# Reordering the end of a transformer prologue: K chunk 2, pair 7's transposes, V tile 1, and the idle products

## The chip, the cores and the metric

The kernel runs on one core of a Trainium2 chip. The metric is the device time of one execution in microseconds, here as the median of several executions. A core has five engines that run their own instruction queues: TensorE (PE, matmuls and transposes), VectorE (DVE), ScalarE (ACT, activations and copies), GpSimd (POOL) and SyncE (SP, which issues transfers).

## The reference

One pre-layernorm transformer block on x of 2048 rows by 512, in bfloat16, with 32 heads of 16 and a gated feed-forward layer of width 1792:

```python
def _A_ref(x, wqkv, wo):                     # H = 32, Dh = 16
    q, k, v = split_heads(x @ wqkv)
    p = softmax(einsum("bhqd,bhkd->bhqk", q, k) * Dh ** -0.5)
    return merge_heads(einsum("bhqk,bhkd->bhqd", p, v)) @ wo

def _B_ref(x, w_gate, w_up, w_down):
    return (sigmoid(x @ w_gate) * (x @ w_up)) @ w_down

h = x + _A_ref(layernorm(x), wqkv, wo)
out = h + _B_ref(layernorm(h), w_gate, w_up, w_down)
```

## The kernel before

The kernel has a prologue, a main loop over groups of score tiles, and a tail for the last query chunk's feed-forward layer.

The main loop (`emit_scores`, `emit_pv`, `emit_fill`) goes through groups of three score tiles of 128 keys by 512 queries. A group's scores are made by TensorE in one of two score buffers of three PSUM banks each, `pss0` and `pss1` in turn; ScalarE takes the exponential of the three banks in one instruction (line L887 in the profile), in some groups VectorE takes one tile of the three (L906 to L919). The product with V (L958) follows some groups later. Between the groups a generator, the filler, hands out the rest of the work one product at a time: V tiles 2 to 15 (L166), the K and Q projections of the other head groups (L171), the output projection and the feed-forward layer. In its first part the filler's V tiles go through two banks, the spare bank (`ps_misc`) and `acc`.

The softmax subtracts no maximum; it subtracts an upper bound of each score, from the norms of q and the largest norm of k. For the first two groups the bound is added to the scores by a second set of three products (L866) with `bnd`; later groups get it as further rows of `QB`, moved there by transfers (L248).

The prologue makes what the first groups need. x arrives in 16 tiles of 128 rows; they are treated in pairs, 0 to 7. For a pair u, `stats(u)` and `apply(u)` normalize on VectorE and GpSimd, `trans(u)` transposes by eight TensorE transposes into one bank and one ScalarE copy into `xnT` (L339, L341). K of head group 0 is made in chunks of 512 rows from two pairs each (`k_chunk`, `k_mm`, L171): a ScalarE square (`square`, L345) for the norms, a ScalarE evacuation into `stg` (`k_copy`, L361), and a transfer that spreads it into `KT` (`k_spread`, L221). The last chunk comes in two halves of 256 rows, half 6 from pair 6 and half 7 from pair 7 (`k_half`, L376; evacuations `half_copy`, L366), so that half 6 does not wait for pair 7. Pair 7's transposes go to two banks, one copied by VectorE, one by ScalarE (`transpose4`, L162, L163). The norms of K chunks 0 to 2 are collected in the spare bank (`norm_part_of`, L350), those of the halves come separately (`norm_half`, L385); `k_max` (L179) reduces each, `k_fold` (L189) and `k_most` bring them together, and `sqrt_bits` and one VectorE instruction make `bnd` (L461). V tiles 0 and 1 are also made here (`v_prod`, L166; `v_cast`, L227).

Three things set the order of the work. The schedule is manual: each engine runs its instructions in the order of the source, and only waits for data and for buffers lie between them. Until the prologue ends, its tiles take six PSUM banks in turn (`pm_tile`); the two score buffers lie on the same six banks, so the first scores wait for the last readers of the prologue's tiles. The spare bank and `acc` are outside of them. And three calls of `spin` (L253) issue TensorE products whose result nobody reads: two before K half 7, two before the last norm, five between group 0's scores (L861) and group 0's bounds (L866).

Of the kernel before, what the change touches and what calls it, by code (L numbers as in the profile page):

```python
# [11 lines left out]
FP32 = mybir.dt.float32  # L12
BF16 = mybir.dt.bfloat16
# [6 lines left out]
def kernel(  # L20
# [11 lines left out]
    nc = tc.nc  # L32
    P = 128
# [8 lines left out]
    QC = 512  # L42
# [24 lines left out]
    ps_misc = ctx.enter_context(tc.tile_pool(name="ps_misc", bufs=1, space=PSUM))  # L67
# [3 lines left out]
    def pm_tile():  # L71
        return pmh["pool"].tile([P, 512], FP32, name="pm")
# [6 lines left out]
    xnT = reg[:, 0:DC * S].rearrange("p (c s) -> p c s", c=DC)  # L79
# [6 lines left out]
    for part in (1, 0, 2):  # L86
        nc.sync.dma_start(out=wqkv_sb[:, :, part * D:(part + 1) * D],
                          in_=wqkv_v[:, :, part * D:(part + 1) * D])
# [7 lines left out]
    ident_bf = const.tile([P, P], BF16)  # L96
# [20 lines left out]
    acc = ps_acc.tile([P, QC], FP32, name="acc")  # L117
# [41 lines left out]
    def transpose4(dst3, src, copy=None):  # L159
        pt = pm_tile()[:].bitcast(BF16)[:, 0:4 * P].rearrange("p (b q) -> p b q", b=4)  # L160
        for b in range(4):
            nc.tensor.transpose(out=pt[:, b, :], in_=src[:, b * P:(b + 1) * P], identity=ident_bf[:])  # L162
        (copy or nc.vector.tensor_copy)(out=dst3, in_=pt)  # L163
# [14 lines left out]
    def k_max(src, dst):  # L178
        nc.vector.tensor_reduce(out=dst[0:src.shape[0], :], in_=src, axis=AX.X, op=ALU.max)  # L179
# [7 lines left out]
    def k_fold(kd, n, col):  # L187
        pc = ps_misc.tile([P, 512], FP32, name="pm")
        nc.tensor.matmul(pc[:, 0:4], lhsT=same[0:n].rearrange("p r h -> p (r h)"), rhs=kd[0:n, :],  # L189
                         start=True, stop=True)  # L190
        k_max(pc[:, 0:4], km2[:, col:col + 1])

    def k_most():
        m2 = small.tile([P, 1], FP32, name="m2")
        nc.vector.tensor_reduce(out=m2[:], in_=km2[:], axis=AX.X, op=ALU.max)
        return m2
# [10 lines left out]
    def q_root(ps, qc):  # L207
        r = slice(32 * qc, 32 * qc + 32)
        sqrt_bits(y0[r, :], ps[r, :])
# [10 lines left out]
    def k_spread(ku, g, cols, eng):  # L220
        eng.dma_start(out=KT[0:P:2, g, cols], in_=ku[64 * (g % 2):64 * (g % 2) + 64, cols])  # L221
# [29 lines left out]
    def spin(ps, rhs, n):  # L251
        for _ in range(n):
            nc.tensor.matmul(ps[:], lhsT=ident_bf[:], rhs=rhs, start=True, stop=True)  # L253
# [10 lines left out]
    def prologue(pro):  # L264
# [12 lines left out]
        for b in range(4):  # L277
            nc.vector.tensor_copy(out=ones_blk[:, b, :, 8 * b:8 * b + 8],
                                  in_=head_of[:].unsqueeze(1).to_broadcast([P, 4, 8]))
# [10 lines left out]
        means, rss, xns, pts, sqs = {}, {}, {}, {}, {}  # L290
# [44 lines left out]
        def trans(u):  # L335
            pts[u] = pm_tile()[:].bitcast(BF16).rearrange("p (b q) -> p b q", b=4)
            for i in range(2):
                for b in range(4):
                    nc.tensor.transpose(out=pts[u][:, b, i * P:(i + 1) * P],  # L339
                                        in_=xns[u][:, i, b * P:(b + 1) * P], identity=ident_bf[:])  # L340
            nc.scalar.copy(out=xnT[:, :, 2 * u * P:(2 * u + 2) * P], in_=pts[u])  # L341

        def square(key, ps, scale=1.0):
            sqs[key] = pro.tile([P, ps.shape[-1]], BF16, name="sq", bufs=3)
            nc.scalar.activation(out=sqs[key][:], in_=ps, func=ACT.Square, scale=scale)  # L345
# [13 lines left out]
        def k_copy(n, ps):  # L359
            cols = slice(n * QC, (n + 1) * QC)  # L360
            nc.scalar.copy(out=ku[:, cols], in_=ps[:])  # L361
            k_spread(ku, 0, cols, nc.sync)

        def half_copy(h):
            w = QC // 2
            nc.scalar.copy(out=ku[:, 3 * QC + h * w:3 * QC + (h + 1) * w], in_=ps3[h][:, 0:w])  # L366
# [3 lines left out]
            square(n, ps[:])  # L370
            k_copy(n, ps)

        def k_half(u):
            ps = pm_tile()
            for c in range(DC):
                nc.tensor.matmul(ps[:, 0:QC // 2], lhsT=wqkv_sb[:, c, D:D + P],  # L376
                                 rhs=xnT[:, c, u * QC // 2:(u + 1) * QC // 2], start=(c == 0), stop=(c == DC - 1))
            square(("half", u), ps[:, 0:QC // 2])
            return ps

        def norm_half(pn, u):
            norm_mm_to(pn[:, 0:QC // 2], sqs[("half", u)])
# [44 lines left out]
        stats(7)  # L427
        apply(6)
        norm_part_of(1)
        trans(6)  # L430
        ps2 = k_mm(2)
        square(2, ps2[:])
        q_root(acc, 0)
        apply(7)
        v1 = v_prod(1, pm_tile())
        norm_part_of(2)
        km4 = small.tile([P, 1], FP32, name="km4")
        k_max(pnp[0:96, :], km4)
        ps3 = [k_half(6)]
        for i, copy in enumerate((nc.vector.tensor_copy, nc.scalar.copy)):  # L440
            t = NT - 2 + i
            transpose4(xnT[:, :, t * P:(t + 1) * P], xns[7][:, i, :], copy)
        kd = k_spots(km4, 96)
        spin(acc, xnT[:, 0, 0:QC], 2)
        ps3.append(k_half(7))
        pn3 = pm_tile()
        norm_half(pn3, 6)
        k_max(pn3[:, 0:QC // 2], km2[:, 1:2])
        k_fold(kd, 96, 0)
        half_copy(1)  # L450
        v_cast(1, v1)
        half_copy(0)
        k_spread(ku, 0, slice(3 * QC, S), nc.sync)
        k_copy(2, ps2)
        spin(acc, xnT[:, 0, 0:QC], 2)
        pn3 = ps_misc.tile([P, 512], FP32, name="pm")
        norm_half(pn3, 7)
        k_max(pn3[:, 0:QC // 2], km2[:, 2:3])
        m2 = k_most()
        sqrt_bits(z0[:], m2[:])  # L460
        nc.vector.tensor_scalar(out=bnd[0:32, :], in0=y0[0:32, :].bitcast(FP32), scalar1=z0[0:32, :].bitcast(FP32),  # L461
# [26 lines left out]
    def v_prod(t, ps):  # L488
        for c in range(DC):
            v_mm(ps, t, c)  # L490
        return ps

    def v_cast(t, ps):
        v_store(t, ps, nc.scalar.copy)
        ready.add(("v", t))
# [351 lines left out]
    def emit_scores(i):  # L847
        group = groups[i]
        n = len(group)
        pss = pss2[i % 2]  # L850
        idle = i >= 3 * FIRST and (state["done"] or state["wait"] > i + CYC)
        pairs = i < FIRST or (i % 2 == 1 or i - i % CYC + 2 in twice) and not idle
        order = list(enumerate(group))
        if pairs and group[0][3] // 2 == group[1][3] // 2:
            order[1:] = order[:0:-1]
        n_of = max(per_bank(u[0]) for u in group)
        parts = [(ui, u, h) for h in range(n_of) for ui, u in order[:2] if h < per_bank(u[0])]
        parts += [(ui, u, h) for ui, u in order[2:] for h in range(per_bank(u[0]))]
        if i < OB:
            for ui, (c, g, k, j) in enumerate(group):  # L860
                nc.tensor.matmul(pss[:, ui, :], lhsT=KT[:, g, k * P:(k + 1) * P], rhs=QB[1][:, j, :],  # L861
                                 start=True, stop=False)
            if i == 0:
                spin(acc, xnT[:, 0, 0:QC], 5)
            for ui, (c, g, k, j) in enumerate(group):
                nc.tensor.matmul(pss[:, ui, :], lhsT=ident_bf[:, j:j + 1].to_broadcast([P, P]), rhs=bnd[:],  # L866
                                 start=False, stop=True)
            parts = []
        for ui, (c, g, k, j), h in parts:
            n_qg = c * NG + g  # L870
            w = CHUNKS[c][1]
            kt = k * per_bank(c) + h
            assert ("k", g // 2) in ready
            h0 = 64 * (j // 2)
            rows = slice(h0, h0 + 64) if pairs else slice(0, P)
            nc.tensor.matmul(pss[:, ui, h * w:(h + 1) * w], lhsT=KT[rows, g, kt * P:(kt + 1) * P],  # L876
                             rhs=QB[n_qg % 2][rows, j, 0:w], start=True, stop=True,
                             tile_position=(h0, 0) if pairs else None)
        for c, g, k, j in group:
            n_qg = c * NG + g  # L880
            if k == (12 if per_bank(c) == 1 else 0) and j == 3 and n_qg + 1 < len(qgs):
                emit_q_rows(n_qg + 1)
                emit_q_bound(n_qg + 1)
        slot = i % 7
        pt = pt4[slot] if slot < 4 else (pt_early if i < GM else pt_late)[slot - 4]
        na = n - 1 if i in split else n
        ex = nc.scalar.activation(out=pt[:, 0:na, :], in_=pss[:, 0:na, :], func=ACT.Exp, scale=DH ** -0.5 / QS)  # L887
        if na < n:
            scratch = scratch_of(i)
            tc.declare_no_dep(exp_bits(pss[:, na, :], *scratch).ins, ex.ins,  # L890
                              reason="both only read, from different banks")
            later(i + 1, lambda: exp_first(*scratch))
            later(i + 2, lambda: exp_second(*scratch))
            later(i + 3, lambda: exp_third(pt[:, na, :], *scratch))
        for ui, u in enumerate(group):
            p_of[u] = pt[:, ui, :]
# [210 lines left out]
```

## Time and profile before

| | |
|---|---|
| median of 3 executions | 961.85 us (961.81 to 962.77) |
| the profiled execution's own time | 963.82 us |
| its span, first to last instruction | 962.0 us |
| mean granted TensorE clock | 0.996 |
| TensorE busy | 843.0 us (88%) |
| VectorE busy | 782.9 us (81%) |
| ScalarE busy | 898.6 us (93%) |
| GpSimd busy | 39.8 us (4%) |
| first exponential of the main loop starts | 31.53 us |

Times in the profile count from the span's start. A row of a timeline gives the start, the duration, the engine, the line of the source, the operation, the tiles written and read, the shape, and how many instructions were merged; in brackets stand the idle time of the engine before it and what ended that. TensorE's records overlap, because products are pipelined. A stretch's row gives each engine's busy time in it and the clock that TensorE was granted, 1.00 being full speed.

### The profile page before, as it was taken

What the parts mean: (1) busy time and instruction counts of PE and PEld (TensorE: products, weight loads), DVE (VectorE), ACT (ScalarE), POOL (GpSimd) and SP (SyncE); (2) the same over time, 40 slices, a digit from 0 to 9 for tenths busy, and PEclk for the clock granted to TensorE, in tenths of its full rate; (3) what the DMA queues carried; (4) which work ended last, traced back from release to release, by engine and by line L of the source; (5) the groups of instructions that cost most, each with busy time, mean ns of one, the idle gap of its engine ahead of it and who ended that gap; (6) DMA issues with size and microseconds to landing.
All of it is one profiled execution on the core that took longest, in us unless ns stands there. A gap on an engine that the chain in (4) does not pass through costs nothing.

```text
span 962.0 us, 17291 instructions
## 1 busy us (share of the span) xinstructions
PE 843.0 (88%) x6442; PEld 337.0 (35%) x6442; DVE 782.9 (81%) x1413; ACT 898.6 (93%) x778; POOL 39.8 (4%) x56
## 2 busy tenths in 40 slices
PE   5998888878888999998788999988788999998988
PEld 2321222222222232222222223222355545456646
DVE  7488888888788888899888888898898778777643
ACT  6789999999999999999999999999998999999862
POOL 4600000000000000000000000000000000000000
PEclk9998999999999999999999999999999999999999
DMA  5102450000003000001001000000010000110010
GB/s 161 24 1 56 115 117 16 16 16 3 15 26 103 16 16 17 19 14 30 9 26 27 16 17 15 19 10 27 16 31 23 17 10 16 27 32 16 9 35 12
DMA packets 37645, 28.45 MB, mean 30 GB/s; under 512 B 17788, under 2 KB 32920, under 8 KB 37560
## 3 DMA queue, kind: packets, MB, share of 16 engines
q1 hardware_dynamic: 37416, 27.22, 10.8%
q8 instruction: 50, 0.82, 0.4%
q14 instruction: 35, 0.29, 0.1%
q10 hardware_dynamic: 144, 0.13, 0.0%
HBM read 20.31 MB, written 2.61 MB: 24 GB/s over the span
## 4 chain that ended last, share of the span: by engine, by line
PE 45%; DVE 22%; ACT 22%; issue 6%; DMA 3%; SPq 1%; POOL 0%; ACTq 0%; DVEq 0%
PE pss L876 21%; ACT pt L887 13%; PE acc L958 8%; PE pm L617 7%; ACT stg L887 4%; ACT wd L887 3%; DVE stg L906 2%; PE pm L633 2%; ACT QTu L887 2%; PE pm L593 2%; DVE pt L919 2%; DVE y L915 2%; PE pm L166 1%; DVE reg L909 1%; DVE reg L630 1%
## 5 line engine op out<-in xcount | busy, mean ns | idle before, releaser
L876 PE MATMUL pss<-QB,KT 128*128 128x512 bf16 (+3 forms) x2554 | 477.5, 338 | 80.2 <-ACT pt L887 40.6
L887 ACT ACTIVATE pt<-pss 128x1536 bf16<-128x1536 f32 (+1 forms) x392 | 502.3, 1364 | 17.1 <-PE pss L876 10.6
L876 PEld LDWEIGHTS <-KT 64*128 64x128 bf16 (+1 forms) x2554 | 179.4, 95 | 341.4 <-issue 233.5
L887 ACT ACTIVATE stg<-pss 128x1536 bf16<-128x1536 f32 (+1 forms) x140 | 183.3, 1359 | 5.0 <-PE pss L876 3.8
L906 DVE TENSOR_SCALAR stg<-pss 128x512 int32<-128x512 f32 x123 | 84.8, 690 | 68.2 <-PE pss L876 60.5
L958 PE MATMUL acc<-pt,Vaug 128*17 128x512 bf16 (+1 forms) x1471 | 112.7, 338 | 2.3 <-DVE pt L919 1.2
L887 ACT ACTIVATE wd<-pss 128x1536 bf16<-128x1536 f32 (+1 forms) x80 | 103.9, 1387 | 3.0 <-PE pss L876 2.6
L887 ACT ACTIVATE QTu<-pss 128x1024 bf16<-128x1024 f32 (+1 forms) x71 | 95.7, 1348 | 1.7 <-PE pss L876 1.3
L912 DVE SCALAR_TENSOR_TENSOR y<-reg 128x512 f32<-128x512 f32 x123 | 85.2, 692 | 4.2
L915 DVE SCALAR_TENSOR_TENSOR y<-y,reg 128x512 f32<-128x512 f32 x123 | 84.3, 685 | 1.1
L958 PEld LDWEIGHTS <-Vaug 128*17 128x17 bf16 x2560 | 49.3, 89 | 95.6 <-issue 81.3
L617 PE MATMUL pm<-reg,reg 128*128 128x512 bf16 (+1 forms) x280 | 57.9, 337 | 7.6 <-DVE reg L630 7.5
L617 PE MATMUL pm<-reg,wu 128*128 128x512 bf16 (+1 forms) x280 | 58.1, 338 | 1.4 <-ACT sg L622 1.1
L633 PE MATMUL pm<-wd,reg 128*128 128x512 bf16 x196 | 55.6, 382 | 1.9 <-DVE ob L638 1.9
L909 DVE TENSOR_SCALAR reg<-stg 128x512 int32<-128x512 int32 x123 | 51.9, 422 | 1.8
L958 PE MATMUL acc<-stg,Vaug 128*17 128x256 bf16 (+1 forms) x564 | 50.6, 326 | 0.7 <-DVE stg L919 0.7
L630 DVE SCALAR_TENSOR_TENSOR reg<-sg,pm 128x512 bf16<-128x512 f32 x56 | 38.2, 683 | 14.2 <-PE pm L617 13.8
L919 DVE SCALAR_TENSOR_TENSOR pt<-y,stg 128x512 bf16<-128x512 f32 x70 | 48.0, 686 | 2.0
L152 POOL TENSOR_TENSOR rs<-ve,pw_neg 128x1 f32<-128x1 f32 x16 | 11.7, 734 | 881.9 <-DVE ve L150 875.3
L622 ACT ACTIVATE sg<-pm 128x512 f32<-128x512 f32 x56 | 36.3, 649 | 10.2 <-PE pm L617 9.8
L906 DVE TENSOR_SCALAR wd<-pss 128x512 int32<-128x512 f32 x45 | 31.0, 689 | 17.0 <-PE pss L876 15.5
L171 PE MATMUL pm<-reg 128*128 128x512 bf16 x124 | 38.2, 397 | 1.4 <-DVE stg L521 0.7
(149 smaller groups left out, 718.0 us busy)
## 6 DMA issues: line engine op xcount, KB each, us to landing
rb_all<-rd SPq DMA_DIRECT2D x96, 64.0 KB
xr<-in_A_x_dram SPq DMA_DIRECT2D x16, 128.0 KB
out_dram<-ob SPq DMA_DIRECT2D x15, 128.0 KB
rb_all<-rd SPq DMA_DIRECT2D x60, 32.0 KB
reg<-in_A_x_dram SPq DMA_DIRECT2D x7, 256.0 KB
KT<-stg SPq DMA_DIRECT2D x7, 256.0 KB
reg<-in_B_w_gate_dram SPq DMA_DIRECT2D x4, 448.0 KB
wu<-in_B_w_up_dram SPq DMA_DIRECT2D x4, 448.0 KB
```

What stands on the lines that cost most here:

```text
L171: nc.tensor.matmul(ps[:], lhsT=wqkv_sb[:, c, w0:w0 + P], rhs=xnT[:, c, n * QC:(n + 1) * QC], start=(c == 0), stop=(c == DC - 1))
L617: nc.tensor.matmul(ps[:, i * w:(i + 1) * w], lhsT=wt[:, c, f * P:(f + 1) * P], rhs=hnT[:, c, 0:w], start=(c == 0), stop=(c == DC - 1))
L630: nc.vector.scalar_tensor_tensor(out=out, in0=a, scalar=1.0, in1=b, op0=ALU.add, op1=ALU.mult)
L633: nc.tensor.matmul(ps[:], lhsT=hT[:, f, tt * P:(tt + 1) * P], rhs=wd[:, f, :], start=(f == 0), stop=(f == FC - 1))
L876: nc.tensor.matmul(pss[:, ui, h * w:(h + 1) * w], lhsT=KT[rows, g, kt * P:(kt + 1) * P], rhs=QB[n_qg % 2][rows, j, 0:w], start=True, stop= ...
L887: ex = nc.scalar.activation(out=pt[:, 0:na, :], in_=pss[:, 0:na, :], func=ACT.Exp, scale=DH ** -0.5 / QS)
L906: return nc.vector.tensor_scalar(out=e_bits, in0=src, scalar1=ONE_BITS, scalar2=0.0, op0=ALU.add, op1=ALU.max)
L909: nc.vector.tensor_scalar(out=e_man, in0=e_bits, scalar1=0x7FFFFF, scalar2=-0x40800000, op0=ALU.bitwise_and, op1=ALU.bitwise_or)
L912: nc.vector.scalar_tensor_tensor(out=e_pol, in0=m, scalar=PA, in1=m, op0=ALU.add, op1=ALU.mult)
L915: nc.vector.scalar_tensor_tensor(out=e_pol, in0=e_pol, scalar=PB, in1=e_man.bitcast(FP32), op0=ALU.add, op1=ALU.mult)
L919: nc.vector.scalar_tensor_tensor(out=dst, in0=e_pol, scalar=PC, in1=e_bits.bitcast(FP32), op0=ALU.add, op1=ALU.mult)
L958: nc.tensor.matmul(acc[32 * j:32 * j + VW, 0:w], lhsT=Vaug[:, kt, 4 * g + j, :], rhs=p[:, h * w:(h + 1) * w], start=(kt == 0), stop=(kt == ...
```

## The change

- K chunk 2's product and square go ahead of pair 6's transposes (before: behind them).
- V tile 1's product is no longer made behind K chunk 2 in one of the six banks; it is made last, behind the last norm, in the spare bank, with its cast behind it.
- Pair 7's transposes go ahead of the product of K half 6 (before: behind it); their copies go ahead of half 6's square, which is taken out of the half's function (`k_mm_half`, `square_half`).
- K chunk 2's evacuation and its spread go ahead of half 7's square and of the two half copies, whose order is now 0, 1 (before: half 1, V tile 1's cast, half 0, then K chunk 2's evacuation).
- The three calls of `spin`, nine products, are removed.

```diff
-        def k_half(u):
+        def k_mm_half(u):
             ps = pm_tile()
             for c in range(DC):
                 nc.tensor.matmul(ps[:, 0:QC // 2], lhsT=wqkv_sb[:, c, D:D + P],
                                  rhs=xnT[:, c, u * QC // 2:(u + 1) * QC // 2], start=(c == 0), stop=(c == DC - 1))
+            return ps
+
+        def square_half(u, ps):
             square(("half", u), ps[:, 0:QC // 2])
-            return ps
...
         norm_part_of(1)
-        trans(6)
         ps2 = k_mm(2)
         square(2, ps2[:])
+        trans(6)
         q_root(acc, 0)
         apply(7)
-        v1 = v_prod(1, pm_tile())
         norm_part_of(2)
         km4 = small.tile([P, 1], FP32, name="km4")
         k_max(pnp[0:96, :], km4)
-        ps3 = [k_half(6)]
+        pt7 = [pm_tile()[:].bitcast(BF16)[:, 0:4 * P].rearrange("p (b q) -> p b q", b=4) for _ in range(2)]
+        for i in range(2):
+            for b in range(4):
+                nc.tensor.transpose(out=pt7[i][:, b, :], in_=xns[7][:, i, b * P:(b + 1) * P], identity=ident_bf[:])
+        ps3 = [k_mm_half(6)]
         for i, copy in enumerate((nc.vector.tensor_copy, nc.scalar.copy)):
             t = NT - 2 + i
-            transpose4(xnT[:, :, t * P:(t + 1) * P], xns[7][:, i, :], copy)
+            copy(out=xnT[:, :, t * P:(t + 1) * P], in_=pt7[i])
         kd = k_spots(km4, 96)
-        spin(acc, xnT[:, 0, 0:QC], 2)
-        ps3.append(k_half(7))
+        square_half(6, ps3[0])
+        ps3.append(k_mm_half(7))
         pn3 = pm_tile()
         norm_half(pn3, 6)
         k_max(pn3[:, 0:QC // 2], km2[:, 1:2])
         k_fold(kd, 96, 0)
+        k_copy(2, ps2)
+        square_half(7, ps3[1])
+        half_copy(0)
         half_copy(1)
-        v_cast(1, v1)
-        half_copy(0)
         k_spread(ku, 0, slice(3 * QC, S), nc.sync)
-        k_copy(2, ps2)
-        spin(acc, xnT[:, 0, 0:QC], 2)
         pn3 = ps_misc.tile([P, 512], FP32, name="pm")
         norm_half(pn3, 7)
         k_max(pn3[:, 0:QC // 2], km2[:, 2:3])
+        v_cast(1, v_prod(1, ps_misc.tile([P, 512], FP32, name="pm")))
         m2 = k_most()
...
                 nc.tensor.matmul(pss[:, ui, :], lhsT=KT[:, g, k * P:(k + 1) * P], rhs=QB[1][:, j, :],
                                  start=True, stop=False)
-            if i == 0:
-                spin(acc, xnT[:, 0, 0:QC], 5)
```

## The prediction

> **What bounds the kernel now.** I read the profile's page first, then the timelines of the engines around the changed lines, then stretches of the clock. The chain that ended last, by engine:
>
> ```profile
> PE 45%; DVE 22%; ACT 22%; issue 6%; DMA 3%; SPq 1%; POOL 0%; ACTq 0%; DVEq 0%
> ```
>
> No engine bounds the whole. The change touches only the prologue's end, so what counts is when the main loop's first steps start, and whether an earlier start is kept. TensorE there (start, duration, line; then the idle time before and what ended it):
>
> ```profile
> 21.51 0.85 PE L339 MATMUL pm<-ident_bf,xn 128*128 128x128 bf16 x8
> 22.20 1.03 PE L171 MATMUL pm<-reg 128*128 128x512 bf16 x4
> 23.06 1.03 PE L166 MATMUL pm<-reg 128*128 128x512 bf16 x4
> 24.02 0.39 PE L350 MATMUL pm<-sq,ones_blk 128*32 128x512 bf16 x1
> 24.34 0.61 PE L376 MATMUL pm<-reg 128*128 128x256 bf16 x4
> 24.79 0.61 PE L162 MATMUL pm<-ident_bf,xn 128*128 128x128 bf16 x8
> 25.23 0.59 PE L253 MATMUL acc<-reg,ident_bf 128*128 128x512 bf16 x2
> 26.07 0.60 PE L376 MATMUL pm<-reg 128*128 128x256 bf16 x4 [0.24 <-ACT reg L163]
> 26.50 0.27 PE L385 MATMUL pm<-sq,ones_blk 128*128 128x256 bf16 x1
> 26.61 0.17 PE L189 MATMUL pm<-kd,same 96*128 96x4 bf16 x1
> 26.64 0.59 PE L253 MATMUL acc<-reg,ident_bf 128*128 128x512 bf16 x2
> 27.36 0.28 PE L385 MATMUL pm<-sq,ones_blk 128*128 128x256 bf16 x1
> 28.88 0.81 PE L861 MATMUL pss<-QB,KT 128*128 128x512 bf16 x3 [1.23 <-issue]
> 29.53 1.24 PE L253 MATMUL acc<-reg,ident_bf 128*128 128x512 bf16 x5
> 30.60 0.81 PE L866 MATMUL pss<-bnd,ident_bf 128*128 128x512 bf16 x3
> ```
>
> In order: pair 6's transposes, K chunk 2, V tile 1, K norm 2, K half 6, pair 7's transposes, two idle products, K half 7, its norms, two idle products, the last norm, group 0's scores, five idle products, group 0's bounds. A row's duration holds the pipeline's tail; from start to start four products cost 0.86 (512 columns) or 0.45 (256), eight transposes 0.44. ScalarE:
>
> ```profile
> 20.11 1.11 ACT L341 COPY reg<-pm 128x1024 bf16<-128x1024 bf16 x1
> ```
> ```profile
> 22.40 1.01 ACT L341 COPY reg<-pm 128x1024 bf16<-128x1024 bf16 x1 [0.69 <-PE pm L339]
> 23.32 0.60 ACT L345 ACTIVATE sq<-pm 128x512 bf16<-128x512 f32 x1
> 25.05 0.38 ACT L345 ACTIVATE sq<-pm 128x256 bf16<-128x256 f32 x1 [1.13 <-PE pm L376]
> 25.43 0.59 ACT L163 COPY reg<-pm 128x512 bf16<-128x512 bf16 x1
> 26.76 0.38 ACT L345 ACTIVATE sq<-pm 128x256 bf16<-128x256 f32 x1 [0.74 <-PE pm L376]
> 27.04 0.37 ACT L366 CAST stg<-pm 128x256 bf16<-128x256 f32 x1
> 27.30 0.61 ACT L227 CAST Vaug<-pm 128x512 bf16<-128x512 f32 x1
> 27.77 0.40 ACT L366 CAST stg<-pm 128x256 bf16<-128x256 f32 x1
> 28.04 0.63 ACT L361 CAST stg<-pm 128x512 bf16<-128x512 f32 x1
> 31.53 5.57 ACT L887 ACTIVATE pt<-pss 128x1536 bf16<-128x1536 f32 x4 [2.87 <-PE pss L866]
> ```
>
> Three things are seen. TensorE waits 1.23 us before group 0's scores although their inputs are old: ScalarE's four evacuations end with K chunk 2's at 28.67, and the score banks overlay the prologue's banks, so scores must wait for it. Next, the five idle products stand between group 0's scores and its bounds; the first exponential (L887) waits 2.87 us for L866 behind them. Last, K half 7 waits until 26.07 for pair 7's copy (25.43 to 26.02), which stood behind half 6's square. From 31.53 the exponentials run gapless, so what starts them earlier starts the loop earlier.
>
> **The change part by part.** I re-time the new order by these rows. Hand-overs come from them too: TensorE to ScalarE 0.10 (24.95 to 25.05), ScalarE to TensorE 0.05 to 0.10 (26.02 to 26.07, 23.92 to 24.02). VectorE's rows:
>
> ```profile
> 22.50 0.73 DVE L332 TENSOR_SCALAR xn<-reg,mvs,rs 128x512 bf16<-128x512 bf16 x2
> ...
> 24.44 0.69 DVE L179 TENSOR_REDUCE km<-pm 96x1 f32<-96x512 f32 x1 [1.20 <-PE pm L350]
> 25.21 0.42 DVE L163 COPY reg<-pm 128x512 bf16<-128x512 bf16 x1
> ...
> 27.68 0.42 DVE L179 TENSOR_REDUCE km<-pm 128x1 f32<-128x256 f32 x1 [0.38 <-PE pm L385]
> ...
> 28.53 0.47 DVE L461 TENSOR_SCALAR bnd<-y,z 32x512 bf16<-32x512 f32 x1
> ```
>
> 1. *K chunk 2 ahead of pair 6's transposes, V tile 1 out of the way.* K chunk 2 needs pair 5's copy, done at 20.11 + 1.11 = 21.22: it starts at 21.27, is issued at 22.13 and ends at 22.30. Its square: 22.40 to 23.00. Pair 6's transposes: 22.13 to 22.74. Their copy now queues behind the square on ScalarE and, with the records' overlap of about 0.1, runs 22.90 to 23.91 (22.40 to 23.41 before): 0.5 later. Who waits for it is K half 6 alone.
>
> 2. *Pair 7's transposes ahead of the halves.* K norm 2 waits for the square: 23.10, then the transposes 23.42 to 24.03 (pair 7 is normalized by 23.23, no wait). ScalarE copies one tile 24.08 to 24.67 right behind pair 6's copy. VectorE first takes K norm 2's maximum (23.52 to 24.21), then copies the other tile 24.29 to 24.71. K half 6 runs at 23.96 beside this. K half 7 starts at 24.71 + 0.06 = 24.77 instead of 26.07: **1.30 us earlier**. The two idle products that lay in this wait (25.23) vanish at no price.
>
> 3. *The two norms.* As before, 26.50 - 26.07 = 0.43 behind the half: 25.20; the last norm another 0.86 on (VectorE's two maxima between): 26.06. ScalarE in that time: half 6's square from 24.67, K chunk 2's evacuation, half 7's square, starts 0.3 to 0.5 apart, the last ends at about 25.88. That is 0.1 before it is wanted; without the overlap of records it would cost 0.1 to 0.2, the first bound of the sum. The second pair of idle products (26.64) lay in the same wait: nothing.
>
> 4. *K chunk 2's evacuation early, the half copies last.* They now end near 26.45, so the 1.23 us wait before the scores goes. What is late next is V tile 1: it stands on TensorE's queue ahead of the scores and waits for the last maximum, because it shares the spare bank with the last norm. The maximum starts 0.32 behind the norm (27.36, 27.68) and takes 0.42: 26.80; V tile 1 starts at 26.86 and is issued by 27.72. From last norm to scores are thus 27.72 - 26.06 = 1.66 us against 28.88 - 27.36 = 1.52: **0.14 us lost**. Behind V tile 1's wait stand the scores and everything after them. Its cast on ScalarE (0.61, from about 27.93 to 28.54) is over before the first exponential can start, and before V tile 2 wants the bank.
>
> 5. *Five idle products gone.* From scores to bounds 30.60 - 28.88 = 1.72 before, 0.65 after (three products, 29.53 - 28.88): **1.07 us**. What is late next could be the bounds themselves (`bnd`), finished 1.64 after the last norm starts (27.36 to 29.00): 27.70, while the products want them at 28.37. Covered by 0.67; if the cover went, it would cost what exceeds that.
>
> Sum: -1.30 + 0.14 - 1.07 = -2.23 us. L866's work starts at 28.37, the first exponential at 29.30.
>
> 6. *Queues passed.* The sync queue sends the same transfers in the same order; the spreads of K chunk 2 and of the halves go earlier. The bound rows of QB[0] follow:
>
> ```profile
> 29.43 1.36 SPq L248 DMA_DIRECT2D QB<-bnd  x2
> ```
> ```profile
> 33.51 0.60 PE L876 MATMUL pss<-QB,KT 64*128 64x512 bf16 x3
> ```
>
> Issued at 29.43, wanted at 33.51: 4.08 us. After: about 27.80 and 31.28, 3.48 us. Should the transfer have needed all of 4.08, group 2 would come 0.60 late; L876 shows no wait, so the price lies between 0 and 0.60. I take 0, as the issuing of both ends 2.7 us before the use; the 0.6 goes into the range. GpSimd's fill of KT for head group 1 moves with `bnd` by 1.3 us and is first read 21 groups into the loop: nothing.
>
> The profiled execution took 963.82 us with a span of 962.0; it becomes 961.6. It stands 1.97 above the median 961.85, which becomes 959.6, provided that the loop moves as a whole: its order is fixed, and nothing in it starts at a given time.
>
> **The clock.** The change removes nine products whose only effect is to keep TensorE busy. Busy microseconds of PE, PEld, DVE, ACT and POOL, then granted clock, DMA share and GB/s, in three stretches:
>
> ```profile
> 25.40:28.80 3.40, 1.88 (x11) 0.80 (x9) 1.87 (x8) 2.52 (x7) 0.00 (x0) 1.00 0.00 0
> 80.00:83.40 3.40, 1.79 (x15) 0.50 (x8) 3.26 (x6) 3.40 (x4) 0.00 (x0) 1.00 0.27 70
> 83.40:90.20 6.80, 6.68 (x28) 1.06 (x28) 4.33 (x8) 5.16 (x5) 0.00 (x0) 0.50 0.23 70
> ```
>
> A stretch in which PE was busy 53% (1.79 of 3.40) was followed by 6.8 us at half clock; one of 55% was not. In my new order the emptiest 3.4 us lie from about 23.45 on: transposes and half 6 1.13, half 7 0.61, its norms 0.10, last norm 0.28, V tile 1's beginning: about 2.15 of 3.4, 63%. That stays above, so I charge nothing. The Trainium skill (TensorE: Matmul & The Clock Gate, "Why this matters for your kernels") has the clock fall after an idle gap of more than about 3 us; by that the price is nothing as well, as no gap of the new order is over 0.6. The second row does not agree with it as a sufficient account: PE was busy more than half of that stretch, and the clock still halved.
>
> **Rivals.**
>
> *A. The half clock at 83.40 goes too.* A start 2.23 us earlier puts other work into the stretch that emptied PE, if the stretches keep their place from the launch. ScalarE was busy 5.16 of 6.80 there and 3.40 of 3.40 just before: 1.64 us more, 961.85 - 2.23 - 1.64 = 958.0. Against it: the median lies 1.97 below the profiled execution, as if the timed runs had no such stretch to lose.
>
> *B. Half of it is given back.* The earlier K half 7 is swallowed by another wait (ScalarE's queue of copies and squares behind pair 6's copy, or group 2's bound rows), and only the five idle products count: 961.85 - 1.07 = 960.8. For: ScalarE becomes the chain from 22.40 to 25.9 with 0.1 to spare. Against: each item is timed by its own row.
>
> *C. The clock halves at the prologue's end: slower.* It decides if the emptiest stretch counts as 53% or less instead of 63%, which it does if transposes (0.6 us of it) count for nothing: 1.55 of 3.4, 46%. Then TensorE, which runs gapless from group 0 on, loses half of 6.8 us: 3.4 - 2.23 = +1.2, 963.0; above 963.8 only if a second such stretch follows. Against: in the only place where it can be seen the stretch without transposes was the one that lost the clock, and a given 3.4 us window has to fall on about 0.4 us of starts. The Trainium skill (same page, "Part 4: PE-mode transpose") says that transposes don't count as busy in the same way; no row here can show that.
>
> *D. The change does not do what it says* is excluded for the order: the schedule is manual, each engine runs its instructions as the source lists them, and nine products are gone from the source.
>
> **How the numbers follow.** Forecast 0.60, A 0.15, B 0.13, C 0.12. The time is the forecast's: 959.6. Its own range is 959.2 to 960.4 (hand-overs 0.4 below; ScalarE's 0.2 and the bound rows' 0.6 above). The range for 8 in 10 takes in A and B with a margin of 0.2: 957.8 to 961.0; C is left out. About 0.2%, 1.9 us, is what a measurement of this kernel can tell from no change: 959.9. Of the forecast's 0.60 some 0.48 lies below that, with A 0.63 faster; B, the rest of the forecast and most of C are within: 0.32; a second half-clock stretch, 0.05 slower.
>
> **What would show it.** K half 7 near 24.8, the last norm near 26.1, V tile 1 near 26.9, scores with no gap behind it, first exponential near 29.3, and the same gapless exponentials after. Wrong would be: a wait of group 0's scores for a ScalarE copy, a wait of L876 for a transfer, V tile 1's cast in front of a waiting exponential, or a clock of 0.50 between 25 and 35 us. If the first exponential is 2.2 earlier and the span is not, the loop does not move as a whole.

## The result, and the profile after

The changed kernel took 958.54 us, the median of five executions (957.69 to 959.50), against 962.77 for the kernel before in five executions beside them (961.81 to 963.50): a ratio of 0.9958 (95% interval 0.9944 to 0.9973). The gain is 4.2 us, where 2.2 were forecast; the time is 1.1 below the forecast's 959.6 and inside the range that was given.

The page of the changed kernel has the same shape: the busy times, the granted clock over the span, and the chain by engine.

```profile
span 956.6 us, 17273 instructions
...
PE 839.0 (88%) x6433; PEld 336.9 (35%) x6433; DVE 783.3 (82%) x1413; ACT 898.2 (94%) x778; POOL 40.0 (4%) x56
...
PEclk9999999999999999999999999999999999999999
...
PE 45%; ACT 24%; DVE 22%; issue 6%; DMA 2%; SPq 1%; POOL 0%; ACTq 0%; DVEq 0%
```

TensorE's 843.0 us have become 839.0, and no slice has lost its clock (mean 1.000 against 0.996). TensorE's timeline at the prologue's end, for the rows that were quoted of before:

```profile
21.92 1.02 PE L171 MATMUL pm<-reg 128*128 128x512 bf16 x4 [0.39 <-ACT reg L341]
22.78 0.61 PE L339 MATMUL pm<-ident_bf,xn 128*128 128x128 bf16 x8
23.69 0.38 PE L350 MATMUL pm<-sq,ones_blk 128*32 128x512 bf16 x1 [0.30 <-ACT sq L345]
24.00 0.62 PE L443 MATMUL pm<-ident_bf,xn 128*128 128x128 bf16 x8
24.59 1.30 PE L376 MATMUL pm<-reg 128*128 128x256 bf16 x8
25.73 0.27 PE L387 MATMUL pm<-sq,ones_blk 128*128 128x256 bf16 x1
25.83 0.17 PE L189 MATMUL pm<-kd,same 96*128 96x4 bf16 x1
26.59 0.28 PE L387 MATMUL pm<-sq,ones_blk 128*128 128x256 bf16 x1 [0.58 <-DVE km L179]
27.38 1.02 PE L166 MATMUL pm<-reg 128*128 128x512 bf16 x4 [0.52 <-DVE km L179]
28.24 0.81 PE L866 MATMUL pss<-QB,KT 128*128 128x512 bf16 x3
28.89 0.81 PE L869 MATMUL pss<-bnd,ident_bf 128*128 128x512 bf16 x3
```

Every step stands where the prediction put it in the order, and the waits are the ones that it named: V tile 1 (L166) waits for the last maximum, the scores follow it without a gap, the bounds follow the scores. But all of it is 0.5 to 0.65 later than forecast, because the first row is: K chunk 2 starts at 21.92, not 21.27, waiting for pair 5's copy. ScalarE's and SyncE's rows:

```profile
20.80 1.07 ACT L341 COPY reg<-pm 128x1024 bf16<-128x1024 bf16 x1
...
29.82 5.57 ACT L890 ACTIVATE pt<-pss 128x1536 bf16<-128x1536 f32 x4 [0.79 <-PE pss L869]
```
```profile
28.25 1.35 SPq L248 DMA_DIRECT2D QB<-bnd  x2
```

That copy starts at 20.80, and at 20.11 before, although nothing ahead of it was changed. TensorE's clock is granted in full only at 17.79 in this execution, at 15.12 in the one before; a repeat of the changed kernel below, with the clock granted at 14.82, has the same copy at 20.06. The first exponential is thus 1.71 us earlier (29.82 against 31.53), not 2.23. The bound rows go out at 28.25, and the products that read them start at 31.79 without a wait.

The two profiled executions are 5.4 us of span apart. The start gives 1.71 of it. Between the exponentials of groups 36 and 40 another 2.42 go, where the kernel before ran at half clock and the changed one doesn't. The rest of the loop gives 0.13 and the tail 1.15. How much of that is the change, and how much the execution, is what the experiments were for.

### The profile page after: what moved, and what is told of

The parts are those of the page before. It is cut to its first block, busy times and chain, and to the rows that moved or that the text cites. A ratio compares the mean times of both kernels' runs of the same rounds, so it can differ in the third digit from the quotient of the medians.

```text
span 956.6 us, 17273 instructions
## 1 busy us (share of the span) xinstructions
PE 839.0 (88%) x6433; PEld 336.9 (35%) x6433; DVE 783.3 (82%) x1413; ACT 898.2 (94%) x778; POOL 40.0 (4%) x56
## 4 chain that ended last, share of the span: by engine, by line
PE 45%; ACT 24%; DVE 22%; issue 6%; DMA 2%; SPq 1%; POOL 0%; ACTq 0%; DVEq 0%
PE pss L879 21%; ACT pt L890 13%; PE acc L961 8%; PE pm L622 7%; ACT stg L890 4%; ACT wd L890 4%; DVE stg L909 2%; PE pm L638 2%; ACT QTu L890 2%; PE pm L598 2%; PE pm L171 2%; DVE y L918 2%; DVE pt L922 2%; DVE reg L912 1%; DVE reg L635 1%
```

## The experiments

Theories beside each other: (1) the change is worth the start of the loop, about 2.3 us, and the rest of the difference is chance; (2) it is worth about 4 us, as something in the loop or the tail hangs on it too; (3) the idle products protect the clock, and their removal is paid for somewhere. "Old" is the order of the kernel before, "new" the changed one. Three groups of runs each had their own executions of the kernel before: medians 962.19 (31 executions), 962.54 (27) and 962.74 (29).

### The idle products and the order, one without the other

The nine idle products removed from the old order:

```diff
-        spin(acc, xnT[:, 0, 0:QC], 2)
...
-        spin(acc, xnT[:, 0, 0:QC], 2)
...
-            if i == 0:
-                spin(acc, xnT[:, 0, 0:QC], 5)
```

> The kernel before with only the nine idle products removed, the old order kept. Theory: the five between group 0's scores and its bounds were on the path, the other four lay in waits; the first exponential comes 1.07 us earlier (30.5 against 31.5, give or take 0.6 for where the clock's warm-up falls) and the time falls by about 1.1 us. Rival (clock): in the old order the idle products kept the emptiest 3.4 us of the prologue at 53% busy; without them it is near 40%, TensorE falls to half clock between 25 and 35 us in this run, and the time rises by up to 2.3 us (3.4 - 1.1). Rival (all of the gain is the idle products): the time falls by 4 us.

Measured: 961.85 (12 executions), ratio 0.9995 (0.9983 to 1.0006). The first exponential starts at 30.61, 0.92 earlier, and the gain is given back at once. Two stretches of this kernel (busy time of PE, PEld, DVE, ACT and POOL, clock, DMA share, GB/s):

```profile
26.64:30.06 3.42, 1.55 (x9) 0.71 (x8) 1.77 (x7) 1.90 (x5) 0.99 (x2) 1.00 0.09 22
30.06:33.47 3.41, 3.41 (x9) 1.22 (x9) 0.00 (x0) 1.83 (x2) 3.41 (x3) 0.50 0.44 95
```

TensorE is busy for 45% of 3.42 us, and then works through group 0 and group 1 at half clock. The same profile loses the clock once more, from 84.67 to 88.08. In 11 of the 12 executions the mean clock is 0.996 or less, which is two such losses or more. In the old order the idle products are worth what they cost.

The same nine put back into the new order, in the same three places:

> The changed kernel with the nine idle products put back where they stood (two before K half 7, two before the last norm, five between group 0's scores and bounds). Theory: 1.07 us slower than the changed kernel, about 959.6; the first exponential at 30.9 instead of 29.8. Rival (the idle products cost nothing in the new order, since bnd is late anyway): 958.5. Rival (the gain is the idle products alone): back at 962.8.

Measured: 960.91 (12), ratio 0.9983 (0.9974 to 0.9992), 2.4 above the new order's 958.54, where 1.07 was the forecast's. TensorE and ScalarE:

```profile
24.46 0.59 PE L253 MATMUL acc<-reg,ident_bf 128*128 128x512 bf16 x2
24.89 0.60 PE L376 MATMUL pm<-reg 128*128 128x256 bf16 x4
...
28.50 1.24 PE L253 MATMUL acc<-reg,ident_bf 128*128 128x512 bf16 x5
```
```profile
30.51 5.57 ACT L894 ACTIVATE pt<-pss 128x1536 bf16<-128x1536 f32 x4 [1.87 <-PE pss L873]
```

The five cost 1.07 again. The two ahead of K half 7, which lay in a wait in the old order, no longer do and cost 0.2 (24.89 against 24.68 in a repeat of the new order below). The rest lies in the tail (below).

### Is it the half clock near 83?

One score product more in each of groups 33 to 37, in the old and in the new order, so that TensorE is busier there:

```diff
+        if 33 <= i < 38:
+            c, g, k, j = group[0]
...
+            nc.tensor.matmul(pss[:, 0, :], lhsT=KT[rows, g, k * P:(k + 1) * P], rhs=QB[(c * NG + g) % 2][rows, j, :],
+                             start=True, stop=True, tile_position=(h0, 0) if pairs else None)
```

> The kernel before with one score product repeated in each of the groups 33 to 37 (the same values written twice), which makes TensorE busier in the stretch from 79 to 85 us that came ahead of the half clock. If half clock there is a usual part of the time before, the time falls by about 2 us, to about 960.7, and the first exponential stays at 31.5. If it was a matter of the one profiled execution, the median stays at 962.8 within 0.4 us. No half clock at 83 us in either case.

> The changed kernel with the same repeated products in groups 33 to 37. If the changed kernel is usually free of the half clock there, nothing: 958.5 within 0.4 us. If it still loses the clock there in some executions (the stretch is as empty as before), the slower ones of its times go, and the median falls by 0.5 to 1 us.

Measured: old 961.81 (12), 0.9993 (0.9985 to 1.0002); new 959.65 (8), 0.9976 (0.9961 to 0.9990). Neither profile has a half clock near 83, and the old order gains 0.4 us, not the 2.4 that the two profiles had shown there. The products have a price that can hide some of a gain: the new order, with nothing to win there, lost 1.1. But two further runs of the old order without them (below) have no half clock near 83 either. So the 2.42 us belonged to that execution more than to the order. Of the twelve profiles without added score products three lose the clock there: this one, the old order without idle products (84.67), and the new order with V tile 1 back (82.63, below).

### The new order again, and each step undone

No edit:

> The changed kernel as it is, timed again beside the kernel before. Theory (the start of the loop, 2.2 to 2.3 us, is what the change brings; the rest of the first comparison was the half clock and a late transfer of the one profiled execution): ratio near 0.9976, about 2.3 us below before, at the same clock. Rival (the change also keeps the clock up later on): 4 us below before, ratio near 0.9958.

Measured: 958.09 (6), 0.9960 (0.9945 to 0.9976): the rival's 4 us, not 2.3. In this execution the clock is granted at 14.82, and the prologue can be laid on the forecast:

```profile
21.30 1.04 PE L171 MATMUL pm<-reg 128*128 128x512 bf16 x4
...
24.68 0.60 PE L376 MATMUL pm<-reg 128*128 128x256 bf16 x4
25.12 0.27 PE L387 MATMUL pm<-sq,ones_blk 128*128 128x256 bf16 x1
...
25.98 0.28 PE L387 MATMUL pm<-sq,ones_blk 128*128 128x256 bf16 x1 [0.58 <-DVE km L179]
26.78 1.02 PE L166 MATMUL pm<-reg 128*128 128x512 bf16 x4 [0.52 <-DVE km L179]
27.64 0.81 PE L866 MATMUL pss<-QB,KT 128*128 128x512 bf16 x3
28.29 0.81 PE L869 MATMUL pss<-bnd,ident_bf 128*128 128x512 bf16 x3
```
```profile
29.21 5.57 ACT L890 ACTIVATE pt<-pss 128x1536 bf16<-128x1536 f32 x4 [0.79 <-PE pss L869]
```

From K half 7 (24.68) on the forecast was 24.77, 25.20, 26.06, 26.86, 27.72, 28.37 and 29.30: each is hit within 0.1. Stretches of the same execution:

```profile
23.40:26.80 3.40, 2.20 (x21) 1.49 (x21) 2.12 (x7) 2.81 (x7) 0.00 (x0) 1.00 0.13 32
77.60:81.00 3.40, 1.86 (x15) 0.50 (x8) 3.26 (x6) 3.40 (x3) 0.00 (x0) 1.00 0.26 75
...
76.25:79.66 3.41, 2.62 (x23) 0.86 (x23) 3.27 (x7) 2.95 (x3) 0.00 (x0) 1.00 0.27 82
79.66:83.08 3.42, 2.47 (x19) 0.60 (x22) 3.35 (x7) 3.42 (x4) 0.00 (x0) 1.00 0.06 15
```

The prologue's emptiest stretch is 65% busy (forecast 63%). The emptiness that cost the kernel before its clock at 83.4 (1.79 of 3.40) is still there, 2.4 earlier (1.86 of 3.40), and the clock stays. In every profile the clock falls a multiple of 3.41 us after it was first granted (in the kernel before at 15.12 and 83.38, 20 times 3.41 apart). On that grid, from 14.82 on, the emptiness falls across two stretches of 77% and 72%, and in the kernel before it filled one of 53%. By these rows it is the phase that decided here, and the change only shifted it by chance; no run set the phase.

V tile 1 back behind pair 7's normalization, its bank one of the six, its cast behind the half copies:

```diff
         apply(7)
+        v1 = v_prod(1, pm_tile())
...
         half_copy(1)
+        v_cast(1, v1)
...
-        v_cast(1, v_prod(1, ps_misc.tile([P, 512], FP32, name="pm")))
```

> The changed kernel with V tile 1 alone put back: its product behind apply(7) in one of the six banks, its cast behind the half copies. Theory: nothing won by the move of V tile 1 itself; its 0.86 us before K norm 2 covers 0.3 us of TensorE's wait there and makes all later steps 0.5 to 0.6 late, while the 0.86 + 0.5 us between last norm and scores go; the scores then wait for the cast on ScalarE: first exponential within 0.3 us of the changed kernel's, time about 0.2 slower. Rival (V tile 1 was what made the scores wait): over 1 us slower.

Measured: 959.14 (10), 0.9969 (0.9958 to 0.9980), 1.05 above the new order in the runs beside it and 0.6 above all its executions. The clock comes late (17.78), so it stands beside the first profile of the new order:

```profile
27.09 0.28 PE L387 MATMUL pm<-sq,ones_blk 128*128 128x256 bf16 x1 [0.58 <-DVE km L179]
28.12 0.81 PE L867 MATMUL pss<-QB,KT 128*128 128x512 bf16 x3 [0.75 <-DMA KT<-stg]
...
48.33 1.02 PE L166 MATMUL pm<-reg 128*128 128x512 bf16 x4 [0.44 <-DVE Vaug L227]
```

```profile
27.28 0.62 ACT L227 CAST Vaug<-pm 128x512 bf16<-128x512 f32 x1
```

The last norm comes 0.50 later (26.59 there), the scores 0.12 earlier (28.24), as V tile 1's product no longer stands ahead of them. The row of the scores names K's spread as what they waited for, 0.75 us; but ScalarE's cast of V tile 1 ends at 27.90, 0.22 before the scores, just as in the kernel before K chunk 2's evacuation ends at 28.67, 0.21 before them. By these rows they wait for the cast, as the expectation said. The step's 0.14 was thus nearly right for the start, and the place at the end is still no worse: the start's 0.12 is lost again and 0.45 more in the loop near 48, where a later V tile waits 0.44 for a cast on VectorE (0.25 in the first profile of the new order).

Pair 7's transposes back behind half 6, half 6's square ahead of their copies:

```diff
+        ps3 = [k_mm_half(6)]
+        square_half(6, ps3[0])
         pt7 = [pm_tile()[:].bitcast(BF16)[:, 0:4 * P].rearrange("p (b q) -> p b q", b=4) for _ in range(2)]
...
-        ps3 = [k_mm_half(6)]
...
-        square_half(6, ps3[0])
```

> The changed kernel with pair 7's transposes behind K half 6 again and half 6's square ahead of their copies. Theory: ScalarE's copy of pair 7 starts behind that square, K half 7 comes 0.9 us later, and so does all that follows: first exponential 0.9 later than in the changed kernel at a like warm-up, time +0.9. Rival (K half 7 is not on the path once K chunk 2's evacuation is early): no change.

Measured: 960.00 (12), 0.9976 (0.9966 to 0.9986), 1.9 above the new order timed beside it. TensorE, then two stretches:

```profile
25.70 0.60 PE L376 MATMUL pm<-reg 128*128 128x256 bf16 x4 [0.67 <-ACT reg L448]
```
```profile
25.02:28.44 3.42, 1.65 (x12) 0.98 (x11) 1.89 (x8) 2.04 (x6) 0.00 (x0) 1.00 0.10 24
28.44:31.85 3.41, 3.41 (x10) 1.21 (x9) 0.26 (x2) 0.70 (x2) 3.15 (x3) 0.50 0.11 28
```

K half 7 waits 0.67 for its copy again and starts 1.0 later than with the transposes first (24.68 in the repeat). With that wait comes a stretch of 48% busy, and the clock halves just as the scores begin: the first exponential comes at 31.74. So in these profiles the reordering keeps the clock without idle products.

Pair 6's transposes back ahead of K chunk 2:

```diff
+        trans(6)
         ps2 = k_mm(2)
         square(2, ps2[:])
-        trans(6)
```

> The changed kernel with pair 6's transposes ahead of K chunk 2 again. Theory: K chunk 2 starts 0.9 us later behind the transposes, its square too, K norm 2 at 24.0 instead of 23.1, and pair 7's transposes stand behind that norm: K half 7 and the first exponential 0.9 us later, time +0.9. Rival (K chunk 2's place makes no difference, as pair 6's copy is earlier by 0.5): no change.

Measured: 959.46 (12), 0.9973 (0.9964 to 0.9983), 1.4 above. TensorE:

```profile
22.18 1.03 PE L171 MATMUL pm<-reg 128*128 128x512 bf16 x4
23.95 0.38 PE L350 MATMUL pm<-sq,ones_blk 128*32 128x512 bf16 x1 [0.75 <-ACT sq L345]
...
25.55 0.60 PE L376 MATMUL pm<-reg 128*128 128x256 bf16 x4 [0.24 <-DVE kd L183]
```

K norm 2 is 0.87 later (23.08 in the repeat), and so is the first exponential, 30.08. With K chunk 2 late, its norm's maximum holds up VectorE, behind it stand the copy of pair 7 and `kd`, and K half 7 comes at 25.55. With one of the two moves undone it comes at 25.55 or 25.70, with both at 24.68, and in the old order at 26.07: the 1.30 of K half 7 needs both.

### Does the loop's start explain the time?

Ten idle products ahead of group 0's scores in the new order, so that the loop starts as late as the old one's:

```diff
+            if i == 0:
+                spin(acc, xnT[:, 0, 0:QC], 10)
```

> The changed kernel with ten idle products (10 x 0.216 = 2.16 us) ahead of group 0's scores, so that its loop starts about when the loop of the kernel before does; all else as in the changed kernel. If the change acts through the start of the loop alone, the first exponential comes 2.16 us later, near 31.4 at an early warm-up, each part of the loop takes as long as before, and at full clock the time is that of the kernel before within 0.5 us. If the new order also saves something behind the start (1 us or more), the time at full clock stays that much below the kernel before.

Two more runs of the old order and one of the new, no edit:

> The kernel before once more, for a second profiled execution and more times. Chance theory: the half clock at 83 us and the late transfer ahead of the tail in the first profiled execution are matters of that execution; this one shows neither, or others in other places, with the first exponential at 31.5 and the same length of every part of the loop. Rival (they belong to the old order): both are there again. Ratio to the kernel before 1.000 within 0.001.

> The kernel before a third time, as the run above: by chance, a span of 958.3 to 959 with neither half clock nor late transfer; by the rival, 962 again with both.

> The changed kernel a third time, beside the others on the same chip: 2.2 to 2.3 us below the kernel before at full clock by the chance theory; 3.6 below if more than the loop's start is saved.

Measured: delayed 962.99 (12), 1.0003 (0.9991 to 1.0015); old 962.01 and 962.64 (12 each); new 959.05 (6), 0.9960 (0.9945 to 0.9975). The ten products take 2.16 us of TensorE:

```profile
28.03 2.32 PE L253 MATMUL acc<-reg,ident_bf 128*128 128x512 bf16 x10
30.19 0.81 PE L868 MATMUL pss<-QB,KT 128*128 128x512 bf16 x3
```

The delayed kernel's first exponential starts at 31.76, and the whole 4 us are gone: at a mean clock of 1.000 it takes 961.30 (4 executions), the old order beside it 961.18 (10). So the new order as such saves nothing behind the start; but 2.16 us of delay cost more than 2.16. Against the repeat of the new order the delayed profile is 3.61 us longer: 2.55 up to the first exponential (its clock came at 17.34, not at 14.82), nothing in the loop, and 1.12 in the tail. The missing part goes with the start or with the idle products.

Of the old order's two further runs one lost the clock at 29.02 and was on time in the tail, the other (span 959.87) kept the clock and was late in the tail. For the latter the chance theory expected neither and a span of 958.3 to 959, the rival both. So the late tail is not an accident of the first profile alone, and it does not hang on the half clock. The new order's third run is 3.7 below the old order beside it, near the 3.6 of its second theory.

Where that part lies is seen in the tail: the output's scaling waits for `rb_all`, the normalizers read back by a transfer. VectorE's timeline has that scaling with its wait. The kernel before:

```profile
932.14 0.43 DVE L939 TENSOR_TENSOR OT<-xs_all,rb_all 128x256 bf16<-128x256 f32 x1 [5.03 <-DMA rb_all<-rd]
```

The old order's third run:

```profile
929.98 0.42 DVE L939 TENSOR_TENSOR OT<-xs_all,rb_all 128x256 bf16<-128x256 f32 x1 [5.24 <-DMA rb_all<-rd]
```

The old order's second run:

```profile
929.85 0.43 DVE L939 TENSOR_TENSOR OT<-xs_all,rb_all 128x256 bf16<-128x256 f32 x1 [3.34 <-DMA rb_all<-rd]
```

The new order with the idle products back:

```profile
930.53 0.42 DVE L946 TENSOR_TENSOR OT<-xs_all,rb_all 128x256 bf16<-128x256 f32 x1 [5.15 <-DMA rb_all<-rd]
```

The new order delayed:

```profile
929.69 0.43 DVE L944 TENSOR_TENSOR OT<-xs_all,rb_all 128x256 bf16<-128x256 f32 x1 [4.79 <-DMA rb_all<-rd]
```

The changed kernel:

```profile
925.91 0.42 DVE L942 TENSOR_TENSOR OT<-xs_all,rb_all 128x256 bf16<-128x256 f32 x1 [3.19 <-DMA rb_all<-rd]
```

Its repeat:

```profile
925.69 0.42 DVE L942 TENSOR_TENSOR OT<-xs_all,rb_all 128x256 bf16<-128x256 f32 x1 [3.50 <-DMA rb_all<-rd]
```

Waits of 4.8 to 5.2 stand against 3.2 to 3.5. Where the transfer is late, the time from the last exponential's start to the end of the span is 32.2 to 32.5, else 31.1: 1.1 to 1.4 us. Over all 14 profiles it is late in four of the six of kernels with nine or ten idle products (not in the old order's second run, nor in that with added score products), half late in one of the eight of kernels without (pair 6's transposes back, 31.56), and on time in the other seven. It is not a late start alone: in the kernel with pair 7's transposes back the loop starts at 31.74, in the old order's second run at 33.22, and in both the tail is on time. It is not the idle products alone either, as two of the six kernels that have them are on time.

## Why the prediction was right or wrong

**The steps of the prologue: right.** At an early clock K half 7, the norms, V tile 1, the scores, the bounds and the first exponential all came within 0.1 of the forecast; the sum of the start was -2.32 against -2.23 (29.21 and 31.53). Pieces tried alone agree: the five idle products 1.07, V tile 1's place 0.12 for 0.14, K chunk 2's order 0.87.

**What was left out of the start: the late clock.** The old order starts its loop at 31.53 to 31.55 whether the clock comes at 15.1 or at 17.3. The new one starts at 29.21 to 29.26 with an early clock (14.8 to 15.6) and at 29.82 with the latest (17.8), since K chunk 2 now stands directly behind pair 5's copy. That takes 0.6 of 2.3 in such an execution.

**The total: too small, and the step that failed is the one that made the profile's 2.23 the median's 2.23**, "provided that the loop moves as a whole: its order is fixed, and nothing in it starts at a given time". The loop does move as a whole: from its first exponential to its last it takes 895.6 to 896.0 us in the four profiles without a half clock and without added score products, two of the new order, the delayed one and one of the old. What does not move with it is the tail's transfer, which the quoted words put at nothing. The five first executions and the two repeats of the new order give 958.54 together (17), the old order's executions in the experiments 962.38 (111): 3.8 us. The granted clock doesn't account for it:

| mean granted clock | old: median (executions) | new: median (executions) |
|---|---|---|
| 1.000 | 961.51 (43) | 957.79 (6) |
| 0.998 | 962.74 (32) | 958.87 (9) |
| lower | 963.48 (36) | 960.05 (2) |

At equal clock the gap is 3.4 to 3.9. A clock lost somewhere is thus the usual case in both orders, 68 of 111 and 11 of 17. Two profiles without any half clock show its parts: the third run of the old order (span 959.87) against the repeat of the new (955.97), 3.90 apart. The start gives 2.34, the loop 0.35 (0.82 lost at group 591, around a longer wait for the same kind of transfer, less 0.45 won at group 381), the tail 1.21. The last two are the terms that the sum lacked, about 1.6 us. The loop's part is not surely the change's: the two profiles of the new order without half clock differ by 0.55 and 0.45 at the same two places. The sentence on the idle products, that those in a wait "vanish at no price", was right for the waits and blind to the tail.

**Rival A**, the half clock at 83.4: absent in the profile after, but as an accident of that execution. Undoing only that (the added score products) moved the old order by 0.4, and with V tile 1 moved back the new order had a half clock at 82.63. Its price was also too low: ScalarE's idle time gave 1.64, the two profiles lie 2.42 apart there. Its 958.0 came near the measured time for another reason, so that the measured 958.54 lies in the stated range by luck: the forecast's own range reached down only to 959.2, and it was this rival that widened it to 957.8. **Rival B**, half given back: false; the 1.30 and the 1.07 both arrived. **Rival C**, the clock lost in the prologue: no profile of the new order shows it, and the mechanism is real one step away. It happened in the old order without idle products, in the new order with pair 7's transposes back, and in one run of the unchanged old order, which the prediction had not considered:

```profile
25.60:29.02 3.42, 1.82 (x12) 0.93 (x11) 1.89 (x9) 2.32 (x6) 0.00 (x0) 1.00 0.00 0
29.02:32.43 3.41, 3.41 (x9) 1.21 (x8) 0.05 (x1) 0.00 (x0) 3.36 (x3) 0.50 0.25 60
```
```profile
33.22 4.14 ACT L887 ACTIVATE pt<-pss 128x1536 bf16<-128x1536 f32 x3 [4.55 <-PE pss L866]
```

There TensorE was 53% busy, idle products included, and the first exponential came at 33.22, 1.7 late. So part of the new order's gain, in some executions, may be that this threatens less: the emptiest 3.4 us at its prologue's end are 65% busy, those of the old order 53%. How often it strikes is not known, as only profiled executions show where a clock was lost.

**What stays open** is why `rb_all` comes late. In the profiles a load of instructions (16 KB packets on the same 16 DMA engines) starts 2.3 to 2.8 us after the first of these transfers is issued where it is late, 2.7 to 4.3 where it is on time, and 3.6 in the half late one, and taking out products shifts where such loads fall. So this load alone does not sort the cases: 2.79 was late, 2.74 was not. In the late case at 2.79 and in the half late one a second load (8 KB, another queue) starts 0.28 and 0.22 us after the first issue; in the other twelve profiles it starts within 0.03 of it. That is argued from traces, not shown: no run moved a load by itself. Most of the missing 1.6 us may thus hang on where instructions lie and not on what they do.

## What to carry to other kernels

Idle products that hold a clock are the price of an order with waits in it: fill the waits with real work first, and then take the products out. Removing the products alone was worth 0.3 us here, reordering alone 1.3, both together 3.8, of which some 1.2 lie in a tail that neither edit touches. Time a moved prologue by its own rows, but before the profile's difference is called the change's, compare many executions at equal granted clock: where one profile's clock was lost (2.4 us here) was chance. And look at the tail even when the edit is at the front: a small transfer there cost 1.2 us, for a reason that these runs do not show.

## What the runs showed of the hardware

The instant at which TensorE's clock is first granted in full lay between 14.8 and 17.8 us over 14 profiles, 14.82 and 17.79 in two executions of the same kernel, and before the tail's end half clock lasted 3.41 (ten times) or 6.83 (once). The Trainium skill (TensorE: Matmul & The Clock Gate, "What's actually happening") describes a free-running window of 3413 ns whose phase differs from run to run; the traces agree.

What had not been expected is how little emptiness is enough. Stretches of 45%, 48% and 53% busy (1.55, 1.65 and 1.82 of 3.42) were followed by half clock without any gap over 1.3 us, while the one of 55% in the kernel before (1.88 of 3.40, from 25.40) was not. Nor is there a sharp bound. The stretch ahead of the second loss in the old order without idle products, then one in the new order with added score products that lost nothing:

```profile
81.26:84.67 3.41, 2.05 (x10) 0.52 (x9) 3.31 (x6) 3.41 (x4) 0.00 (x0) 1.00 0.16 49
```
```profile
793.04:796.45 3.41, 1.83 (x22) 0.74 (x21) 3.34 (x7) 2.79 (x3) 0.00 (x0) 1.00 0.04 8
```

The first is 60% busy and its longest gap is 0.75 us; the second is 54% busy with one gap of 1.58. So TensorE's busy share in a stretch does not settle alone whether the clock is kept, and what else counts stays open. The same page of the Trainium skill says that throughput drops are avoided by having no idle gaps over about 3 us ("Why this matters for your kernels"), which these runs show to be not enough; its section "A second HAM failure mode: psum-queue depth-cycling" tells of a clock that is lost through frequent short idling, and the stretch from 81.26 on, with three gaps of 0.19 to 0.75 us, agrees with that.
